# Attention with top-k and an MLP on one core: reads of the hidden products behind the score copies, GpSimd's part of the MLP later

## The chip, the cores and the metric

The kernel runs on one core of a Trainium2 chip. The metric is the device time of one execution in microseconds, as the median over several executions. A profiled execution gives, beside its own time, the span from its first to its last instruction and a record of every instruction on the engines: TensorE (PE, with its weight loads PEld), VectorE (DVE), ScalarE (ACT), GpSimd (POOL) and SyncE (SP), which issues the DMA transfers.

## The reference

For 8 batches and 8 heads, with 576 positions and 64 elements a head, attention keeps for every query the 32 largest scores. Its output, 4608 tokens of 512, goes through an MLP with a smoothed ReLU (SmeLU, beta 1) of width 2048. All is float32.

```python
scores = scale * np.matmul(q, k.transpose(0, 1, 3, 2))
kth = np.partition(scores, -top_k, axis=-1)[..., -top_k:-top_k + 1]
scores = np.where(scores >= kth, scores, -1000000000.0)
attn = np.exp(scores - np.max(scores, axis=-1, keepdims=True))
attn = attn / (np.sum(attn, axis=-1, keepdims=True) + 1e-09)
x = np.matmul(attn, v)          # then (B,H,S,D) -> (B*S, H*D)
h = x @ w_in
g = np.where(h >= 1, h, np.where(h <= -1, 0.0, (h + 1) ** 2 / 4))
out = g @ w_out
```

## The kernel before

**Steps.** Attention is cut into 144 steps. A step holds 128 queries of two heads, as two halves of a tile with 576 scores each. Four steps (the four pairs of heads) complete one chunk of 128 tokens for the MLP; there are 36 chunks. The order of four engines (TensorE, VectorE, ScalarE, GpSimd) is written out by hand: the Python loop over steps `m`, with 7 slots in each, issues the instructions, and every engine runs its own in that order. SP's order is left to the scheduler.

**One step.** TensorE makes the scores `sp` (L358) in two halves, each in a PSUM tile of tag "a", of which there are two. ScalarE copies them to `s` (L359). VectorE finds the 32nd largest: pairwise maxima and minima of the two halves of a row (`more` and `less`, L372), rounds of eight maxima and replacements (L392, L420, L428, L439, L446, L379), and a merging scan `kth` (L451). ScalarE makes the exponentials `e` (L395) from the negative maximum `nmax` (L393). VectorE masks them and sums them (L458), and takes the reciprocal `rz` (L404) early in the next step. GpSimd multiplies `e` by it (L411, twice a step) and writes two columns of `excess` (L414). ScalarE splits the weights into 16-bit halves (L488), SP stores them and reads them back transposed as `wT` (L490, L492), TensorE multiplies with the values into `po` (L506), and ScalarE copies that to the chunk's `xT` (L519).

**The MLP.** For each chunk, `hidden(x)` makes eight matrix products into one PSUM tile `ph` (L539), then ScalarE reads it twice, into `r` (L543) and `g` (L550), then GpSimd bounds `r` to 1 (L555), squares it (L556) and adds it to `g` (L557). There are two buffers of `r` and eight of `g`. `po` shares the three PSUM tiles of `ph`. `final(f)` multiplies `g` with `w_out` into `py` (L562), and comes four groups of `hidden` later (`LAG`); at the end ScalarE copies `y` (L565) and SP stores it.

**What sets the order around the change.** The MLP's pieces wait in a list `pending`. At the end of each slot `advance` takes pieces from it, as many as a share worked out from the work left allows, by planned costs and not by measured ones. In slot 2 of every even step, after the early steps in which weights are converted, the scores of two later steps are issued with the value products of two earlier steps between them (L794 to L800). Ahead of them a loop (L796) takes pieces until the last one is not a `hidden`. The divisions of the step before (L411) are issued in slot 0.

A second program for other input values is built after the first and started by a flag (L844). It isn't executed here.

Of the kernel before, what the change touches and what calls it, by code (L numbers as in the profile page):

```python
# [17 lines left out]
ALU = mybir.AluOpType  # L18
# [8 lines left out]
def kernel(  # L27
# [10 lines left out]
    nc = tc.nc  # L38
# [17 lines left out]
    GROUP = 2  # L56
# [51 lines left out]
    n_pieces = NK * DFF // WC + NF * DM // WC  # L108
# [68 lines left out]
    def run(ctx, paired):  # L177
# [350 lines left out]
            return [(i * TL, (i + 1) * TL, out[r0 + i * S + SM:r0 + (i + 1) * S, :]) for i in range(2)]  # L528

        def mlp(xT, rows, pool, last):  # L530
            gs, group = {}, 1 if last else GROUP
            py = []

            def hidden(x):
                ph = ps.tile([P, group, P], F32, name="ph", tag="ph", bufs=3)
                for i in range(group):
                    f = x * group + i
                    for kk in range(NK):
                        nc.tensor.matmul(ph[:, i], w_in[:, kk, f * P:(f + 1) * P], xT[:, kk],  # L539
                                         start=(kk == 0), stop=(kk == NK - 1))  # L540

                r = pool.tile([P, GROUP, P], F32, name="r", bufs=2)[:, 0:group]
                nc.scalar.activation(r, ph, AF.Relu, bias=half, scale=0.5 * unit)  # L543
                gs[x] = g = pool.tile([P, GROUP, P], F32, name="g", bufs=2 * LAG)[:, 0:group]
                if last:
                    nc.scalar.activation(g, ph, AF.Relu, bias=minus_half, scale=0.5 * unit)
                    nc.vector.scalar_tensor_tensor(out=r, in0=r, scalar=1.0, in1=r, op0=ALU.min, op1=ALU.mult)
                    nc.vector.tensor_tensor(out=g, in0=r, in1=g, op=ALU.add)
                    return
                nc.scalar.activation(g, ph, AF.Relu, bias=minus, scale=unit)  # L550
                if converted < n_pieces and x % 2:
                    nc.scalar.activation(r, r, AF.Square)
                    nc.gpsimd.tensor_scalar(r, r, 1.0, 0.0, ALU.min, ALU.max)
                else:
                    nc.gpsimd.tensor_scalar(r, r, 1.0, 0.0, ALU.min, ALU.max)  # L555
                    nc.gpsimd.tensor_tensor(out=r, in0=r, in1=r, op=ALU.mult)  # L556
                nc.gpsimd.tensor_tensor(out=g, in0=r, in1=g, op=ALU.add)  # L557

            def final(f):
                if f == 0:  # L560
                    py.append(ps.tile([P, DM], F32, name="py", tag="py", bufs=1))
                nc.tensor.matmul(py[0], gs[f // group][:, f % group], w_out[:, f, :], start=(f == 0), stop=(f == NF - 1))  # L562
                if f == NF - 1:
                    y = (late or words).tile([P, DM], F32, name="y", bufs=1)
                    nc.scalar.activation(y, py[0], AF.Copy, scale=unit)  # L565
                    for p0, p1, dst in rows:
                        nc.sync.dma_start(out=dst, in_=y[p0:p1])

            behind = []
            while pending and pending[-1][3]:
                behind.insert(0, pending.pop())
            for x in range(NF // group + LAG):
                if x < NF // group:
                    pending.append((NK * group, needed(x * group + group - 1, False), partial(hidden, x), False))
                if x < LAG:
                    for _ in range(min(GROUP + 1, len(behind))):
                        pending.append(behind.pop(0)[0:3] + (False,))
                else:  # L580
                    for f in range((x - LAG) * group, (x - LAG + 1) * group):
                        pending.append((DM // P, needed(f, True), partial(final, f), x >= NF // group))
# [14 lines left out]
        n = len(steps)  # L597
# [6 lines left out]
        pending = deque()  # L604
        total, spent = len(chunks) * (NK * NF + NF * DM // P), 0
        converted, inspected, due = 0, 0, 0.0

        begun, pipe = 0, deque()

# [23 lines left out]
        taken = None  # L633

        def take():

            nonlocal spent, due, pe_time, taken
            cost, pieces, work, _ = pending[0]
            if pieces > converted or usable[pieces] > pe_time + 0.5:
                return False  # L640
            pending.popleft()
            due -= cost
            spent += cost
            pe_time += cost * UNIT_TIME
            work()
            taken = work.func
            return True
# [62 lines left out]
        def begin_until(m):  # L710
            for x in range(len(state), m + 1):
                begin_at(x)
# [31 lines left out]
        for m in range(n + 2):  # L744
            early = converted < n_pieces
# [21 lines left out]
            for slot in range(SLOTS):  # L767
                now = start + (dve_time - start) * (slot + 1) / SLOTS
                for _ in range(parts[slot]):
                    next(top_k, None)  # L770
                if m < n and converted < n_pieces:
                    if slot in now_converting:
                        convert(now)
                elif slot == 3 and late is not None:
                    if m % 2:
                        inspect()
                    elif paired:
                        load(late, inspected, 1, 2)
                if slot == 1 and 1 <= m <= n and state[m - 1]["by_tensor"]:
                    pe_time = max(pe_time, done[m - 1] + 2.0) + 1.0  # L780
                    transpose_w(state[m - 1])
                    ready_at[m - 1] = pe_time + 1.8
                if slot == 3 and 1 <= m <= n and state[m - 1] is not None and not state[m - 1]["by_tensor"]:
                    move_w(state[m - 1])
                    ready_at[m - 1] = done[m - 1] + 15.0
                if slot == 3:
                    finish_turns()
                if slot == 2 and m == n and paired:
                    judge(ps, att)
                if slot == 2 and (early or m == first_late or m >= n - 1):  # L790
                    values_until(m)
                if m == 0 and slot in (1, 2):
                    next(first)
                if slot == 2 and not early:  # L794
                    if m % 2 == 0:
                        while pending and taken is not None and taken.__name__ == "hidden" and take():  # L796
                            pass
                    begin_until(min(m + 2, len(state)))
                    values_until((m - 2) // 2 * 2)
                    begin_until(m + 3 - m % 2)  # L800
                if slot == 4 and early:
                    begin_at(m + 2)
                if slot == (6 if early else 1):
                    queries(m + (3 if early else 5))
                    if (m < n and prep is None and next_keys < B and steps[m][0] == next_keys - 1 and steps[m][1] >= 1
                            and (next_keys > 1 or converted == n_pieces)):
                        prep = (turned_keys_of if next_keys > 1 else keys_of)(next_keys)
                    if prep is not None and (m % 2 == 0 or next_keys == 1):
                        got = next(prep, None)
                        pe_time += 0.5 if next_keys < 2 else 0.0  # L810
                        if got is None:
                            prep, next_keys = None, next_keys + 1
                        else:
                            keys[next_keys] = got
                            value_loads = got.get("loads", value_loads)
                    elif value_loads is not None:
                        next(value_loads, None)
                if paired and early and spent == 0 and not pending:
                    rest = ps.tile([P, NT, P], F32, name="rest", tag="py", bufs=1)
                    for i in range(5):  # L820
                        nc.tensor.transpose(rest[:, i % NT, :], ident, ident)
                advance((EARLY_SHARE if early else share) / SLOTS if m < n else 32.0, now)
            for _ in (top_k if top_k is not None else ()):
                pass
        while pending:
            advance(32.0, pe_time + 8.0)
        order.__exit__(None, None, None)


# [12 lines left out]
    with ExitStack() as inner:  # L842
        run(inner, True)
# [31 lines left out]
```

## Time and profile before

| what | us |
|---|---|
| median of 3 executions | 1488.8 (1488.8 to 1494.17) |
| profiled execution, own time | 1492.76 |
| its span | 1490.9 |
| TensorE busy | 1437.7 |
| VectorE busy | 1411.9 |
| ScalarE busy | 1157.7 |
| GpSimd busy | 949.8 |
| step to step in the middle, four steps | 37.77 to 38.60 |

Busy time is the union of an engine's instructions. Matrix products are pipelined and their ends are modelled, so that TensorE's busy time can hold short pauses. In rows of groups the columns are: line, engine, operation, output and inputs with sizes, count, busy us, mean ns of one, and idle time of the engine just before them with what ended it. In rows of the timeline they are: start, length, engine, line, operation, names, sizes, count, and in brackets the idle time before with its releaser.

### The profile page before, as it was taken

What the parts mean: (1) busy time and instruction counts of PE and PEld (TensorE: products, weight loads), DVE (VectorE), ACT (ScalarE), POOL (GpSimd) and SP (SyncE); (2) the same over time, 40 slices, a digit from 0 to 9 for tenths busy, and PEclk for the clock granted to TensorE, in tenths of its full rate; (3) what the DMA queues carried; (4) which work ended last, traced back from release to release, by engine and by line L of the source; (5) the groups of instructions that cost most, each with busy time, mean ns of one, the idle gap of its engine ahead of it and who ended that gap; (6) DMA issues with size and microseconds to landing.
All of it is one profiled execution on the core that took longest, in us unless ns stands there. A gap on an engine that the chain in (4) does not pass through costs nothing.

```text
span 1490.9 us, 32088 instructions
## 1 busy us (share of the span) xinstructions
PE 1437.7 (96%) x10755; PEld 1044.0 (70%) x10755; DVE 1411.9 (95%) x4392; ACT 1157.7 (78%) x2221; POOL 949.8 (64%) x1310
## 2 busy tenths in 40 slices
PE   7998899999999999999999999999999999999998
PEld 5765677777777777677767776767777777777675
DVE  6989999999999999999999999999999999999912
ACT  7986877888788877787778888788778887777632
POOL 3474576666676666666766667666666666677730
PEclk8999999999999999999999999999999999999999
DMA  8533567766677777886667786887677876665400
GB/s 253 193 120 107 149 170 203 198 182 170 170 202 197 192 184 204 204 209 177 170 186 199 198 200 173 208 214 182 170 201 187 203 202 168 161 167 138 149 25 17
DMA packets 510319, 260.94 MB, mean 175 GB/s; under 512 B 460992, under 2 KB 469184, under 8 KB 510144
## 3 DMA queue, kind: packets, MB, share of 16 engines
q1 hardware_dynamic: 510144, 258.80, 66.0%
q8 instruction: 87, 1.43, 0.4%
q14 instruction: 88, 0.72, 0.2%
HBM read 62.91 MB, written 102.63 MB: 111 GB/s over the span
## 4 chain that ended last, share of the span: by engine, by line
PE 65%; DVE 13%; ACT 10%; DMA 5%; POOL 4%; issue 3%; SPq 0%; POOLq 0%; ACTq 0%; DVEq 0%
PE py L562 26%; PE ph L539 23%; PE sp L358 8%; PE po L506 6%; DVE more L379 3%; ACT halves L488 2%; DVE e L458 2%; DMA rows<-halves 2%; ACT e L395 2%; POOL r L556 2%; DMA wT<-rows 2%; ACT r L543 1%; DVE more L372 1%; POOL g L557 1%; DVE tops L420 1%
## 5 line engine op out<-in xcount | busy, mean ns | idle before, releaser
L539 PEld LDWEIGHTS ph<-xT,w_in 128*128 128x128 f32 x4608 | 547.1, 192 | 102.3 <-issue 78.6
L539 PE MATMUL ph<-xT,w_in 128*128 128x128 f32 x4608 | 555.6, 276 | 2.3 <-ACT g L550 1.4
L562 PE MATMUL py<-w_out,g 128*128 128x512 f32 x1152 | 542.3, 597 | 0.7 <-ACT y L565 0.7
L555 POOL TENSOR_SCALAR r<-r 128x256 f32<-128x256 f32 x276 | 172.4, 625 | 401.3 <-ACT r L543 401.3
L379 DVE MATCH_REPLACE8 more<-tops,more 128x288 f32<-128x288 f32 x864 | 375.0, 437 | 0.0
L562 PEld LDWEIGHTS py<-w_out,g 128*128 128x128 f32 x1152 | 199.5, 191 | 165.1 <-issue 159.8
L488 ACT COPY halves<-e 128x1152 uint16<-128x1152 uint16 x268 | 293.7, 1143 | 19.9 <-DMA rows<-halves 12.5
L411 POOL TENSOR_SCALAR e<-e,rz 128x576 f32<-128x576 f32 x268 | 251.6, 949 | 10.0 <-DVE rz L404 10.0
L458 DVE SCALAR_TENSOR_TENSOR e<-s,kth,e 128x577 f32<-128x577 f32 x288 | 252.5, 912 | 0.5 <-ACT e L395 0.4
L543 ACT ACTIVATE r<-ph,half 128x256 f32<-128x256 f32 (+1 forms) x296 | 135.9, 459 | 145.2 <-PE ph L539 101.5
L557 POOL TENSOR_TENSOR g<-r,g 128x256 f32<-128x256 f32 x280 | 221.0, 789 | 22.0
L395 ACT ACTIVATE e<-s,nmax 128x576 f32<-128x576 f32 x288 | 222.6, 773 | 4.7
L556 POOL TENSOR_TENSOR r<-r 128x256 f32<-128x256 f32 x276 | 201.6, 730 | 23.0
L359 ACT ACTIVATE s<-sp 128x576 f32<-128x576 f32 x288 | 171.6, 649 | 52.6 <-PE sp L358 51.7
L358 PE MATMUL sp<-kT,qT 64*128 64x288 f32 x1024 | 163.9, 438 | 18.0 <-ACT s L359 12.4
L358 PEld LDWEIGHTS sp<-kT,qT 64*128 64x128 f32 x1024 | 89.0, 189 | 91.7 <-issue 35.3
L506 PE MATMUL po<-wT,v_in 128*64 128x128 f32 x2048 | 138.3, 276 | 6.4 <-DMA wT<-rows 5.6
L506 PEld LDWEIGHTS po<-wT,v_in 128*64 128x64 f32 x2048 | 113.2, 137 | 30.7 <-issue 11.4
L372 DVE TENSOR_TENSOR more<-s 128x576 f32<-128x576 f32 x144 | 122.5, 850 | 8.3 <-ACT s L359 8.3
L550 ACT ACTIVATE g<-ph,minus 128x256 f32<-128x256 f32 x280 | 129.8, 464 | 0.0
L420 DVE MAX8 tops<-more 128x8 f32<-128x288 f32 x288 | 125.4, 443 | 0.0
L392 DVE MAX8 tops<-more 128x8 f32<-128x288 f32 x288 | 116.4, 443 | 0.0
(92 smaller groups left out, 1378.3 us busy)
## 6 DMA issues: line engine op xcount, KB each, us to landing
rows<-halves SPq DMA_DIRECT2D x134, 576.0 KB, 3.4
lines<-parts SPq DMA_DIRECT2D x48, 256.0 KB, 2.7
q_in<-in_q_dram SPq DMA_DIRECT2D x32, 256.0 KB, 3.9
v_in<-in_v_dram SPq DMA_DIRECT2D x32, 256.0 KB, 4.3
out_dram<-y SPq DMA_DIRECT2D x32, 256.0 KB, 4.1
raw<-in_moe_w_in_dram SPq DMA_DIRECT2D x32, 256.0 KB, 3.3
raw<-in_moe_w_out_dram SPq DMA_DIRECT2D x32, 256.0 KB, 3.5
kT<-in_moe_w_in_dram SPq DMA_DIRECT2D x8, 512.0 KB, 4.8
```

The lines of the kernel that those rows point to most:

```text
L358: nc.tensor.matmul(*x, start=True, stop=True)
L379: nc.vector.match_replace(out=st["rest"][:, i, :], in_to_replace=eight(st["tops"], i, r - 8), in_values=src[:, i, :], imm_value=LOWEST)
L395: nc.scalar.activation(e[:, i, :], s[:, i, :], AF.Exp, bias=nmax[:, i:i + 1])
L411: nc.gpsimd.tensor_scalar(st["e"][:, i, :], st["e"][:, i, :], rz[:, i:i + 1], 1.0, ALU.mult, ALU.mult)
L458: nc.vector.scalar_tensor_tensor(out=st["all"][1][:, i, :], in0=st["all"][0][:, i, :], scalar=last[i], in1=st["all"][1][:, i, :], op0=ALU. ...
L488: nc.scalar.copy(halves[:, :, i * S:(i + 1) * S], st["e"][:, i, :].bitcast(U16).rearrange("p (k t) -> p t k", t=2))
L506: nc.tensor.matmul(po[j * D:(j + 1) * D], v_in[:, h, c, :] if c < NT else v_tl[0][:, h, :], wT[:, block(j, c)], start=(c == 0), stop=(c == ...
L539: nc.tensor.matmul(ph[:, i], w_in[:, kk, f * P:(f + 1) * P], xT[:, kk], start=(kk == 0), stop=(kk == NK - 1))
L555: nc.gpsimd.tensor_scalar(r, r, 1.0, 0.0, ALU.min, ALU.max)
L556: nc.gpsimd.tensor_tensor(out=r, in0=r, in1=r, op=ALU.mult)
L557: nc.gpsimd.tensor_tensor(out=g, in0=r, in1=g, op=ALU.add)
L562: nc.tensor.matmul(py[0], gs[f // group][:, f % group], w_out[:, f, :], start=(f == 0), stop=(f == NF - 1))
```

## The change

`hidden` no longer issues ScalarE's two reads itself: it puts them into a list `reads`, which is emptied at once unless `holding` is set. `holding` is set in slots 1 and 2 of even steps after the early ones, until the scores of slot 2's first `begin_until` are issued; then the held reads follow. The loop that takes pieces ahead of the scores stops when three reads are held. GpSimd's three instructions become `bound`, which goes to a queue `bounds`. An entry is issued at the end of a slot when more than two further slots have been done since it was made, or before the next read when more than one is queued, or when a `final` needs its `g`; in early steps and after the last attention step at the end of each slot. Arithmetic and instruction counts stay as they are.

```diff
             def hidden(x):
...
+                reads.append(partial(read, x, ph))
+                if not holding:
+                    issue_reads()
+
+            def read(x, ph):
+                while len(bounds) > 1:
+                    bounds.popleft()[1]()
                 r = pool.tile([P, GROUP, P], F32, name="r", bufs=2)[:, 0:group]
                 nc.scalar.activation(r, ph, AF.Relu, bias=half, scale=0.5 * unit)
                 gs[x] = g = pool.tile([P, GROUP, P], F32, name="g", bufs=2 * LAG)[:, 0:group]
...
                 nc.scalar.activation(g, ph, AF.Relu, bias=minus, scale=unit)
-                if converted < n_pieces and x % 2:
+                by_act = converted < n_pieces and x % 2
+                if by_act:
                     nc.scalar.activation(r, r, AF.Square)
-                    nc.gpsimd.tensor_scalar(r, r, 1.0, 0.0, ALU.min, ALU.max)
-                else:
-                    nc.gpsimd.tensor_scalar(r, r, 1.0, 0.0, ALU.min, ALU.max)
+                bounds.append((slots_done, partial(bound, x, r, g, by_act)))
+
+            def bound(x, r, g, by_act):
+                nc.gpsimd.tensor_scalar(r, r, 1.0, 0.0, ALU.min, ALU.max)
+                if not by_act:
                     nc.gpsimd.tensor_tensor(out=r, in0=r, in1=r, op=ALU.mult)
                 nc.gpsimd.tensor_tensor(out=g, in0=r, in1=g, op=ALU.add)
+                whole_g.add(x)
 
             def final(f):
...
+                if f // group not in gs:
+                    issue_reads()
+                while f // group not in whole_g:
+                    bounds.popleft()[1]()
...
+        def issue_reads():
+            while reads:
+                reads.pop(0)()
...
+                holding = not early and m % 2 == 0 and slot in (1, 2) and m < n
                 if slot == 2 and not early:
                     if m % 2 == 0:
-                        while pending and taken is not None and taken.__name__ == "hidden" and take():
+                        while len(reads) < 3 and pending and taken is not None and taken.__name__ == "hidden" and take():
                             pass
                     begin_until(min(m + 2, len(state)))
+                    holding = False
+                    issue_reads()
                     values_until((m - 2) // 2 * 2)
                     begin_until(m + 3 - m % 2)
...
                 advance((EARLY_SHARE if early else share) / SLOTS if m < n else 32.0, now)
+                slots_done += 1
+                while bounds and (early or m >= n or bounds[0][0] < slots_done - 2):
+                    bounds.popleft()[1]()
...
         while pending:
             advance(32.0, pe_time + 8.0)
+            while bounds:
+                bounds.popleft()[1]()
```

More of the change, by code (lines that the diff above doesn't have):

```diff
@@ L530, in mlp @@
         def mlp(xT, rows, pool, last):
-            gs, group = {}, 1 if last else GROUP
+            gs, group, whole_g = {}, 1 if last else GROUP, set()
             py = []
@@ L548, in hidden @@
                     nc.vector.tensor_tensor(out=g, in0=r, in1=g, op=ALU.add)
+                    whole_g.add(x)
                     return
                 nc.scalar.activation(g, ph, AF.Relu, bias=minus, scale=unit)
-                if converted < n_pieces and x % 2:
+                by_act = converted < n_pieces and x % 2
+                if by_act:
                     nc.scalar.activation(r, r, AF.Square)
-                    nc.gpsimd.tensor_scalar(r, r, 1.0, 0.0, ALU.min, ALU.max)
-                else:
-                    nc.gpsimd.tensor_scalar(r, r, 1.0, 0.0, ALU.min, ALU.max)
+                bounds.append((slots_done, partial(bound, x, r, g, by_act)))
+            def bound(x, r, g, by_act):
+                nc.gpsimd.tensor_scalar(r, r, 1.0, 0.0, ALU.min, ALU.max)
+                if not by_act:
                     nc.gpsimd.tensor_tensor(out=r, in0=r, in1=r, op=ALU.mult)
                 nc.gpsimd.tensor_tensor(out=g, in0=r, in1=g, op=ALU.add)
+                whole_g.add(x)
             def final(f):
@@ L606, in run @@
         converted, inspected, due = 0, 0, 0.0
+        reads, bounds, holding, slots_done = [], deque(), False, 0
+        def issue_reads():
+            while reads:
+                reads.pop(0)()
         begun, pipe = 0, deque()
```

## The prediction

> **What bounds the kernel now.** I read the page first, then waits by engine in the steady middle, then two equal stretches side by side, then the instructions of one of them.
>
> ```profile
> PE 1437.7 (96%) x10755; PEld 1044.0 (70%) x10755; DVE 1411.9 (95%) x4392; ACT 1157.7 (78%) x2221; POOL 949.8 (64%) x1310
> ```
>
> TensorE (PE) and VectorE (DVE) are both nearly full, so the page alone doesn't say which sets the end. The waits from 200 to 1410 us do: VectorE has none at all, and TensorE has this one of size (us in total, times, longest), while ScalarE (ACT) waits often for TensorE and for GpSimd (POOL):
>
> ```profile
> PE sp L358 <- ACT s L359: 10.4, 16, 1.4
> ACT r L543 <- POOL g L557: 36.1, 26, 2.3
> ```
>
> So VectorE's own instructions, back to back, carry the time from about 170 us to 1420 us, and nothing that shortens a wait elsewhere can shorten that, unless VectorE's instructions themselves get shorter. They can. L458, L372 and L451 of VectorE have these durations (min/median/max ns):
>
> ```profile
> L458 DVE SCALAR_TENSOR_TENSOR e<-s,kth,e x288: 799/811/1815, 25.8 to 1420.8; 128x577 f32<-128x577 f32 x144
> L451 DVE TENSOR_TENSOR_SCAN kth<-tops,seconds x144: 190/200/1269, 25.3 to 1419.7; 128x25 f32<-128x25 f32 x144
> ```
>
> From 200 to 1410 us the means are 912 ns for L458 (x252) and 846 and 805 ns for the two forms of L372 (x126 each, median 746); L451 has 289 over the whole run. Mean less median: 252 x 0.101 = 25.5 us, 126 x (0.100 + 0.059) = 20.0 us, 126 x 0.089 = 11.2 us, together 57 us in 126 steps, or 0.45 us a step. What lengthens them stands in the timeline below: GpSimd runs at that moment.
>
> Four attention steps make one period, with one chunk of MLP in it. Two pairs of periods (us, then busy us of PE, PEld, DVE, ACT, POOL):
>
> ```profile
> 752.46:791.06 38.60, 37.91 (x274) 27.23 (x273) 38.60 (x121) 30.01 (x59) 26.93 (x37) 1.00 0.70 194
> 791.06:829.65 38.59, 37.89 (x273) 27.21 (x273) 38.59 (x121) 31.87 (x61) 26.92 (x37) 1.00 0.72 193
> 1023.45:1061.22 37.77, 37.77 (x274) 27.30 (x273) 37.77 (x121) 30.60 (x59) 24.15 (x36) 1.00 0.70 172
> ```
>
> The same work takes 38.6 us in one and 37.77 in the other. TensorE's busy time is the same within 0.14 us; the long period has 0.69 us of TensorE idle. 37.77 is thus about what TensorE needs with no stall. From the reciprocal at 205.05 us to that at 1395.91 there are 31 periods in 1190.86 us, mean 38.41; if all took 37.77 the stretch would be 1170.9, 20 us less. That is the most the change can give there while TensorE does the same work.
>
> The place of the 0.69 us, in the second of these periods: ScalarE, TensorE, GpSimd, VectorE.
>
> ```profile
> 817.08 0.47 ACT L543 ACTIVATE r<-ph,half 128x256 f32<-128x256 f32 x1 [1.13 <-POOL g L557]
> 817.81 1.19 ACT L359 ACTIVATE s<-sp 128x576 f32<-128x576 f32 x2
> ...
> 818.51 1.30 PE L358 MATMUL sp<-kT,qT 64*128 64x288 f32 x8 [0.70 <-ACT s L359]
> ...
> 814.50 1.74 POOL L556 TENSOR_TENSOR r<-r 128x256 f32<-128x256 f32 x1
> 816.31 0.73 POOL L557 TENSOR_TENSOR g<-r,g 128x256 f32<-128x256 f32 x1
> 818.89 1.97 POOL L411 TENSOR_SCALAR e<-e,rz 128x576 f32<-128x576 f32 x2
> ...
> 818.28 0.70 DVE L451 TENSOR_TENSOR_SCAN kth<-tops,seconds 128x25 f32<-128x25 f32 x1
> 819.31 0.93 DVE L458 SCALAR_TENSOR_TENSOR e<-s,kth,e 128x577 f32<-128x577 f32 x1
> 820.18 1.29 DVE L458 SCALAR_TENSOR_TENSOR e<-s,kth,e 128x577 f32<-128x577 f32 x1
> ```
>
> The third read of hidden products waits for a free r (two buffers, the first still with GpSimd, whose L556 took 1.74 us against a usual 0.61 because VectorE's two L372 ran). The score copies stand behind that read, though their products were done at 815.5; the next scores find no bank and TensorE waits. Over on VectorE, L451 loses 0.50 us, and L458 0.12 and 0.48, to GpSimd's L557 and the two L411.
>
> **What the Trainium skill says.** "SBUF — State Buffer", section "Who interferes with whom": a VectorE instruction with two SBUF inputs contends with a GpSimd instruction that reads SBUF; whichever issues first holds the pair for its whole length and the other blocks. The trace agrees: L372, L451 and L458 all have two inputs and stretch, and GpSimd's L556 stretches to 1.74 when it comes second. VectorE's maxima and replacements, with one input, keep 437 to 443 ns as group means. "PSUM — Partial Sum Buffer", section "Engine vs sequencer instructions": the queues of ScalarE, VectorE and GpSimd are strict first in, first out. The trace agrees: copies whose input was done at 815.5 start at 817.81, behind the read.
>
> **The change part by part.** No instruction is added or removed on any engine. The orders of TensorE and VectorE are the same in both programs. In the program that runs, ScalarE's order changes in 33 places, once in four steps: one pair of reads (r and g, 0.47 us each; two pairs at the first place) goes behind two score copies and ahead of the copies of po. GpSimd's changes in 33 places: the last of three parts "bound" (0.40 + 0.61 + 0.73 = 1.74 us alone) goes behind the two L411 and L414 of the step. Most other bounds keep their rank, because a bound is delayed only past what is issued within three slots, and that is mostly nothing. On SP one key load changes place with one row store and one weight load with one transposition, once each, where the first rows are stored (around 170 us). Such transfers land in 2.8 to 4.7 us, and both moved ones feed later steps, so I put them at nothing; if the keys or the weights came late, it would cost one such landing, 5 us at most.
>
> ScalarE's move, in the period shown: ScalarE is free at 815.95, the scores done at 815.48, so the copies run 815.95 to 817.14 and not 817.81 to 819.00. The second scores can start when po ends, at 817.81: the 0.70 us are gone. The third read follows at 817.14 (r is free at 817.04) and ends at 818.0, hardly later than now; the copies of po come 0.9 us earlier. Behind the held read stand only those; the next products that need its bank start at 820.70, so 2 us cover it. Without the cover TensorE would wait what the read is late. Sum over the middle: 10.4 us of TensorE's stalls, 16 of them.
>
> GpSimd's move: L411 starts at 817.04 instead of 818.89, 1.85 us earlier (its reciprocal was done at 811.65). Alone it takes 2 x 0.74, to 818.5. VectorE's L451 at 818.28 then waits 0.23 instead of 0.50. L414 and the moved bound come next, 818.7 to about 820.7, and now they meet L458: I take up to 0.2 for the first and 0.35 for the second (what is left of L556's 0.61 when VectorE's own changeover is taken off, as L411's 0.74 costs 0.48 in the rows above). Sum 0.8 against 1.1: 0.3 us less. Bounds of this unknown: 0.7 less, if the moved bound always comes second to VectorE; 0.4 more, if it also pushes the following bound, now starting at 824.6, in front of L372. I take 0.3, since a bound is shorter than an L411. x 33 = 10 us on VectorE. What the moved bound makes late is its g, by about 2.4 us; its py stands four groups later, in periods with eight groups, some 19 us, which hides it. Its r is wanted by the read at 823 to 824 and free near 820.8.
>
> Both sums are about 10 us, on the two engines that pace each other, so they do not add: 10 us come off. The profiled execution has a span of 1490.9 and a time of 1492.8, 1.9 more; it would go to 1482.8. It lies 4.0 above the median of the runs shown, between 1488.8 and 1494.17, so from the median: 1488.8 - 10 = 1478.8, said as 1479. The last 70 us, with VectorE nearly done, and the first 160, where weights are converted, keep their order and their time.
>
> **The rivals.** *Full recovery:* with the stalls gone, TensorE runs ahead of VectorE until L411 ends before L372 in every step; then VectorE falls under 37.77 and TensorE sets the pace: 20 us less, 1469. For it: the long and short periods differ only in how the engines lie to each other. Against: VectorE has no wait at all even in the short ones.
>
> *Contention only moves:* VectorE sets the end alone, and what L451 no longer loses L458 and L372 lose to the moved bound; TensorE's stall was cover that VectorE never felt: 1489, give or take 5. For it: VectorE never waited on the scores that come earlier. Against: L411 is the longest GpSimd instruction in these collisions and it leaves the place where they are worst.
>
> *Slower:* TensorE's loop, freed of its 0.70 us, carries GpSimd earlier against VectorE. In the second and third step of the period the reciprocals end at 792.5 and 802.0, L372 starts at 795.22 and 804.72, and L411 comes just behind it (795.69, 805.26) and yields. If GpSimd comes more than 0.5 us earlier, L411 is first, and L372 waits up to 0.74 once or twice instead of the 0.37 and 0.44 now: about 0.4 more a step, 0.8 a period, less the 0.3 above: 0.5 x 31 = 15 us more, 1504. It decides if the lead settles between 0.5 and 1.5 us; past 1.5, L411 is through before L372 begins. For it: the stall removed is larger than 0.5. Against: a lead that makes VectorE slower grows further, and leaves the bad stretch.
>
> **How the numbers follow.** Forecast (8 to 13 us less) 0.40, full recovery (over 13) 0.15, contention only moves 0.28, slower 0.17. Half a per cent, 7.4 us, is about what a measurement of this kernel can tell from no change: faster 0.55, same 0.28, slower 0.17. The likeliest time is 1479, its own range 1475 to 1482. The range for 8 in 10 runs from full recovery, 1470, to just past no change, 1496, and leaves out most of the slower rival and the extreme of the recovery. It takes in 0.7 less a period (1466 if TensorE let it, which it doesn't) and, in part, 0.4 more (1502).
>
> **What would show it.** Right: TensorE's wait for the score copies falls from 10.4 us to under 2; ScalarE's wait of reads for GpSimd stays near 36; L411 starts about 1.9 us earlier in the fourth step; the mean of L451 falls under 0.25 us; VectorE still has no waits, and periods are near 38.1. Wrong: VectorE's means of L372 rise over 0.88 (the slower rival), or the 57 us of contention stay while the stall goes (it only moves), or VectorE starts to wait for scores (full recovery).

## The result, and the profile after

The changed kernel takes 1482.18 us (median of 6, 1478.1 to 1484.11) against 1490.64 us (median of 6, 1488.8 to 1494.17): ratio 0.9936, 95% interval 0.9918 to 0.9953, or 8.5 us less of a forecast 10. The profiled executions have spans of 1490.9 and 1482.2 us.

The first part of the page after (busy us, share of the span, instructions):

```profile
PE 1435.8 (97%) x10755; PEld 1044.6 (70%) x10755; DVE 1403.9 (95%) x4392; ACT 1158.0 (78%) x2221; POOL 926.6 (63%) x1310
```

VectorE is busy 8.0 us less and TensorE 1.9 us less, with the same instructions. Of TensorE's waits from 200 to 1410 us, and then ScalarE's for GpSimd there (us in total, times, longest), these are the two longest of TensorE and those that answer to the ones shown of before (L550 is now the first read, L567 and L568 are the square and the addition):

```profile
PE po L514 <- DMA wT<-rows: 3.0, 2, 1.9
PE po L506 <- ACT parts L283: 2.5, 1, 2.5
...
PE sp L358 <- ACT s L359: 0.7, 1, 0.7
...
ACT r L550 <- POOL g L568: 3.4, 5, 1.0
ACT r L550 <- POOL r L567: 2.6, 2, 1.3
```

TensorE's wait for the copies went from 10.4 to 0.7 us. Not all of that is gain: its other waits, for transposed weights (`wT`) and for the parts of keys that ScalarE makes (L283) above all, grew from 4.1 to 7.5 us between 200 and 1380 us, so that its waits there fell by 6.3 us, from 14.5 to 8.2. The 1.9 us of busy time go with a granted clock of 0.992 in the profile after and 0.991 before.

Now the same place in a period of the changed kernel: ScalarE, TensorE, GpSimd, VectorE.

```profile
847.33 1.04 ACT L283 COPY parts<-k_block 128x1024 uint16<-128x1024 uint16 x1
848.26 1.20 ACT L359 ACTIVATE s<-sp 128x576 f32<-128x576 f32 x2
849.50 0.47 ACT L550 ACTIVATE r<-ph,half 128x256 f32<-128x256 f32 x1
...
849.85 0.39 PE L506 MATMUL po<-wT,v_tail 128*64 128x128 f32 x4
850.17 1.24 PE L358 MATMUL sp<-kT,qT 64*128 64x288 f32 x8
...
846.93 1.73 POOL L567 TENSOR_TENSOR r<-r 128x256 f32<-128x256 f32 x1
848.74 0.73 POOL L568 TENSOR_TENSOR g<-r,g 128x256 f32<-128x256 f32 x1
849.45 1.47 POOL L411 TENSOR_SCALAR e<-e,rz 128x576 f32<-128x576 f32 x2
...
850.70 0.28 DVE L451 TENSOR_TENSOR_SCAN kth<-tops,seconds 128x25 f32<-128x25 f32 x1
851.31 0.81 DVE L458 SCALAR_TENSOR_TENSOR e<-s,kth,e 128x577 f32<-128x577 f32 x1
852.05 1.16 DVE L458 SCALAR_TENSOR_TENSOR e<-s,kth,e 128x577 f32<-128x577 f32 x1
```

GpSimd's square is held as long as before (1.73 us; VectorE's two L372 ran from 846.77), but the copies no longer stand behind the read that waits for it: they follow L283, and the second scores start where `po` ends, without a wait. L411 starts 5.52 us after the reciprocal (843.93), with 5.53 forecast and 7.38 before. VectorE loses 0.08 on L451 and 0.35 on the second L458, where it lost 1.1.

From the reciprocal at 202.28 us to that at 1385.19 there are again 31 periods, 38.16 us each (38.41 before). About the last ten run at what the prediction called TensorE's need, as these two do (us, then busy us of PE, PEld, DVE, ACT, POOL; the third number from the end is the granted clock):

```profile
1082.99:1120.76 37.77, 37.77 (x273) 27.29 (x273) 37.77 (x122) 30.12 (x60) 25.02 (x36) 1.00 0.77 200
1120.76:1158.53 37.77, 37.77 (x273) 27.29 (x273) 37.77 (x121) 31.80 (x62) 25.04 (x36) 1.00 0.74 192
```

The longest of the others takes 40.73 us. It holds a wait of 2.52 us for the parts of the keys, and behind it a stretch in which TensorE was granted little more than half its clock:

```profile
639.00:642.40 3.40, 3.40 (x26) 2.08 (x22) 3.40 (x11) 1.79 (x5) 2.94 (x4) 0.57 0.69 261
```

### The profile page after: what moved, and what is told of

It reads as the page before. It is cut to its first block, busy times and chain, and to the rows that moved or that the text cites. A ratio compares the mean times of both kernels' runs of the same rounds, so it can differ in the third digit from the quotient of the medians.

```text
span 1482.2 us, 32086 instructions
## 1 busy us (share of the span) xinstructions
PE 1435.8 (97%) x10755; PEld 1044.6 (70%) x10755; DVE 1403.9 (95%) x4392; ACT 1158.0 (78%) x2221; POOL 926.6 (63%) x1310
## 4 chain that ended last, share of the span: by engine, by line
PE 80%; DVE 10%; DMA 4%; ACT 4%; issue 2%; SPq 1%; ACTq 0%; DVEq 0%
PE ph L539 30%; PE py L578 29%; PE sp L358 9%; PE po L506 9%; DVE more L379 2%; DMA rows<-halves 2%; DVE e L458 2%; DMA wT<-rows 1%; PE po L514 1%; DVE more L372 1%; DVE tops L420 1%; DVE tops L428 1%; DVE tops L392 1%; PE pw L473 1%; ACT halves L488 1%
## 5 line engine op out<-in xcount | busy, mean ns | idle before, releaser
L565 POOL TENSOR_SCALAR r<-r 128x256 f32<-128x256 f32 x280 | 166.9, 596 | 413.4 <-ACT r L550 409.7
L568 POOL TENSOR_TENSOR g<-r,g 128x256 f32<-128x256 f32 x280 | 241.6, 863 | 22.0
L458 DVE SCALAR_TENSOR_TENSOR e<-s,kth,e 128x577 f32<-128x577 f32 x288 | 246.9, 893 | 0.1
L411 POOL TENSOR_SCALAR e<-e,rz 128x576 f32<-128x576 f32 x268 | 235.9, 890 | 13.2 <-DVE rz L404 13.2
L550 ACT ACTIVATE r<-ph,half 128x256 f32<-128x256 f32 (+1 forms) x296 | 136.1, 460 | 107.8 <-PE ph L539 99.7
L567 POOL TENSOR_TENSOR r<-r 128x256 f32<-128x256 f32 x276 | 183.1, 663 | 23.0
L372 DVE TENSOR_TENSOR more<-s 128x576 f32<-128x576 f32 x144 | 124.1, 862 | 6.0 <-ACT s L359 6.0
L420 DVE MAX8 tops<-more 128x8 f32<-128x288 f32 x288 | 125.4, 443 | 0.0
L372 DVE TENSOR_TENSOR less<-s 128x576 f32<-128x576 f32 x144 | 117.7, 817 | 0.0
```

Of the source, the lines that this page charges most:

```text
L372: nc.vector.tensor_tensor(out=x, in0=s[:, :, 0:SH], in1=s[:, :, SH:S], op=op)
L411: nc.gpsimd.tensor_scalar(st["e"][:, i, :], st["e"][:, i, :], rz[:, i:i + 1], 1.0, ALU.mult, ALU.mult)
L458: nc.vector.scalar_tensor_tensor(out=st["all"][1][:, i, :], in0=st["all"][0][:, i, :], scalar=last[i], in1=st["all"][1][:, i, :], op0=ALU. ...
```

## The experiments

Two causes were left side by side by the prediction: TensorE's stall at the scores (A), and GpSimd's divisions leaving the place where they lengthen VectorE's instructions (B). Ratios are to the kernel before on the same chip, with 95% intervals. "Stall" is TensorE's wait for the score copies from 200 to 1380 us (10.4 us before), and "all waits" is the sum of its waits there (14.5 us before). These and the busy times are of one profiled execution each; the ones of the changed kernel, act_only and after_r3 were the slowest of their six.

| run | ratio | interval | stall | all waits | VectorE busy |
|---|---|---|---|---|---|
| changed kernel | 0.9936 | 0.9918 to 0.9953 | 0.7 | 8.2 | 1403.9 |
| act_only | 0.9937 | 0.9916 to 0.9957 | 0.8 | 10.1 | 1404.2 |
| pool_only | 0.9937 | 0.9918 to 0.9956 | 4.3 | 8.4 | 1403.1 |
| before_r3 | 0.9942 | 0.9922 to 0.9962 | 1.6 | 8.6 | 1402.2 |
| after_r3 | 0.9928 | 0.9907 to 0.9948 | 0 | 10.4 | 1403.3 |
| after_write_only | 0.9921 | 0.9896 to 0.9945 | 0.5 | 7.5 | 1353.5 |
| before_write_only | 0.9921 | 0.9895 to 0.9946 | 1.4 | 7.1 | 1357.7 |
| after_dve_less | 0.9925 | 0.9901 to 0.9949 | 0 | 7.3 | 1391.4 |
| before_dve_less | 0.9995 | 0.9981 to 1.0008 | 5.6 | 11.5 | 1388.7 |
| before_r3_dve | 0.9935 | 0.9918 to 0.9952 | 0.7 | 7.4 | 1372.7 |
| after_pe_less | 0.9883 | 0.9859 to 0.9907 | 1.2 | 21.2 | 1401.4 |
| before_pe_less | 0.9953 | 0.9940 to 0.9966 | 7.7 | 26.3 | 1408.1 |
| after_pe_less_wo | 0.9806 | 0.9778 to 0.9834 | 0 | 15.7 | 1353.9 |

**Each part alone.** In act_only ScalarE has the changed order and GpSimd the old one; in pool_only it is the other way round. The orders of TensorE and VectorE are the same in all four.

```diff
 act_only, against the changed kernel
-                bounds.append((slots_done, partial(bound, x, r, g, by_act)))
+                bound(x, r, g, by_act)
 pool_only, against the changed kernel
-                holding = not early and m % 2 == 0 and slot in (1, 2) and m < n
+                holding = False
```

> ScalarE's order of the changed kernel, GpSimd's order of the kernel before: the reads are held, each bound is issued with its read. Theory A (the gain comes from TensorE's stall at the scores): the stall of 10.4 us goes, time 8 to 9 us under before, like the whole change. Theory B (the gain comes from GpSimd's L411 leaving the place where it blocks L451 and L458): the stall goes too, but VectorE's means of L451 (289 ns) and L458 (912) stay, and the time stays within 3 us of before.

> GpSimd's order of the changed kernel, ScalarE's order of the kernel before: no read is held, bounds come later. Theory A: TensorE's wait for the score copies stays near 10 us and the time within 3 us of before. Theory B: mean of L451 falls to about 233 ns as in the changed kernel, VectorE is busy 6 to 8 us less, time 6 to 9 us under before, stall or not.

Each part alone brings the whole gain, within what intervals of 3 us either way can tell, so neither theory stands as it was put. ScalarE's part does what A said, and VectorE is busy 7.7 us less in it although GpSimd's order is the old one; that already speaks against B. GpSimd's part leaves 4.3 of the 10.4 us of stall, yet its time can't be told from the others'; all of TensorE's waits together are 8.4 us in it, about as many as in the changed kernel. Its mean of L451 is 264 ns from 200 to 1380 us, not the 233 that B expected, and the same as in act_only.

**The wait for r taken away, in the old orders.** Three buffers of `r`, and seven of `g` for room, in the kernel before and in the changed one.

```diff
-                r = pool.tile([P, GROUP, P], F32, name="r", bufs=2)[:, 0:group]
+                r = pool.tile([P, GROUP, P], F32, name="r", bufs=3)[:, 0:group]
...
-                gs[x] = g = pool.tile([P, GROUP, P], F32, name="g", bufs=2 * LAG)[:, 0:group]
+                gs[x] = g = pool.tile([P, GROUP, P], F32, name="g", bufs=2 * LAG - 1)[:, 0:group]
```

> The kernel before with three buffers of r instead of two (and seven of g instead of eight, for room); all orders as before. The third read no longer waits for GpSimd. Theory A: TensorE's stall falls under 2 us and the time falls like that of the ScalarE part alone, 8 us. Theory B: the stall falls, L411 keeps its place behind three bounds, L451 and L458 stay as long, time within 3 us of before.

> The changed kernel with three buffers of r and seven of g. Its stall at the scores is already 0.7 us, so theory A gives nothing more, within 2 us of the changed kernel. Theory B: nothing either, unless the freer reads shift GpSimd against VectorE; 0 to 4 us either way.

One more buffer gives the kernel before what the reordering gives, with no instruction moved, and gives the changed kernel nothing more that could be measured. The third read's wait for `r` is thus enough as the root of the loss. B said within 3 us of before: wrong, although L411 is where it was in GpSimd's order.

**GpSimd with almost nothing to read.** The three instructions of a bound and the two divisions of a step become fills of the same tiles, so that bounding, squaring, adding and dividing are left out. Only L414, of two columns, still reads.

```diff
-                    nc.gpsimd.tensor_scalar(st["e"][:, i, :], st["e"][:, i, :], rz[:, i:i + 1], 1.0, ALU.mult, ALU.mult)
+                    nc.gpsimd.memset(st["e"][:, i, :], 0.001)
...
-                nc.gpsimd.tensor_scalar(r, r, 1.0, 0.0, ALU.min, ALU.max)
+                nc.gpsimd.memset(r, 0.5)
                 if not by_act:
-                    nc.gpsimd.tensor_tensor(out=r, in0=r, in1=r, op=ALU.mult)
+                    nc.gpsimd.memset(r, 0.25)
-                nc.gpsimd.tensor_tensor(out=g, in0=r, in1=g, op=ALU.add)
+                nc.gpsimd.memset(g, 0.5)
```

> The changed kernel with GpSimd's three instructions of a bound and its two divisions of a step replaced by fills of the same tiles (nothing is read; the bounding, squaring, adding and dividing are left out); orders as changed. VectorE then meets no reader but L414: its means go to L451 0.20, L458 0.81, L372 0.74 us. If TensorE's work (37.77 us a period) is the floor, the time falls 8 to 14 us under the changed kernel, to about 1470. If VectorE alone sets the pace, it falls by the whole contention, 50 us, to about 1430.

> The same fills in the kernel before, orders as before. If what the change removes is lost only through the port that VectorE and GpSimd share, this one is as fast as the changed kernel with fills, within 2 us, the stall at the scores included, since L556 is then never held. If the order of ScalarE has a worth of its own, it stays 5 to 10 us slower than that.

VectorE's work falls by 50 us and the time stays at that of the changed kernel, in either order. 1430 us didn't come, nor 1470: the 31 periods take 38.0 us each in after_write_only, and only some 18 of them lie near 37.77. VectorE now waits openly, which it did neither in the kernel before nor in the changed one:

```profile
DVE e L458 <- ACT e L395: 38.8, 45, 3.3
```

This is after_write_only from 200 to 1380 us. So the 50 us by which GpSimd lengthened VectorE's instructions in the changed kernel did not set its time. And with GpSimd hardly ever held, the order of ScalarE has no worth of its own: both versions have the ratio 0.9921.

**Less of VectorE's work.** One of the two maxima of `less` is left out in each step (for one half of the tile the merging scan then reads a list that isn't renewed), in both kernels.

```diff
-                for i in range(2):
+                for i in range(1):
                     nc.vector.max(out=seconds[:, (1 - i) * SPLIT + 1:(1 - i) * SPLIT + 9], in_=st["less"][:, i, :])
```

> The changed kernel with one of the two maxima of less in each step left out (L446, 144 x 0.37 = 53 us of VectorE). TensorE's pace: no more than 12 us less than the changed kernel, periods at 37.77. VectorE's pace: 45 to 53 us less.

> The kernel before with the same maximum left out (53 us of VectorE). If VectorE set the pace before the change: 40 us or more under before. If TensorE with its stalls sets it and VectorE only follows: VectorE's instructions grow longer against GpSimd by about what was taken, and the time lies between the changed kernel's (0.994 of before) and before's, by how much of the 10.4 us stall is left where the engines then lie.

Taking 53 us from the engine that never waits brings nothing in either kernel. In the changed one VectorE's busy time falls only from 1403.9 to 1391.4 us: some 40 of the 53 us come back as longer instructions. From 200 to 1380 us, L458 and L451 there (count | busy us, mean ns | idle before):

```profile
L458 DVE SCALAR_TENSOR_TENSOR e<-s,kth,e 128x577 f32<-128x577 f32 x250 | 238.6, 989 | 1.7 <-ACT e L395 1.6
...
L451 DVE TENSOR_TENSOR_SCAN kth<-tops,seconds 128x25 f32<-128x25 f32 x124 | 48.5, 391 | 0.0
```

and the same two rows of the changed kernel with its full work:

```profile
L458 DVE SCALAR_TENSOR_TENSOR e<-s,kth,e 128x577 f32<-128x577 f32 x248 | 213.2, 895 | 0.0
...
L451 DVE TENSOR_TENSOR_SCAN kth<-tops,seconds 128x25 f32<-128x25 f32 x123 | 28.5, 232 | 0.0
```

The kernel before without the maximum is not as fast as the changed one without it: 0.9995 against 0.9925. Its waits from 200 to 1380 us show what a readier VectorE does to the old order:

```profile
ACT r L543 <- POOL g L557: 29.4, 25, 1.9
ACT r L543 <- POOL r L556: 12.5, 10, 1.4
...
PE sp L358 <- ACT s L359: 5.6, 17, 0.4
```

And its chain of waits in one period of the middle (start, us, what) goes through the read that waits for GpSimd into the copies and the scores:

```profile
770.54 0.45 ACT r L543
771.06 0.69 POOL r L555
771.84 1.00 POOL r L556
772.91 0.74 POOL g L557
773.68 0.47 ACT r L543
774.15 0.36 ACT g L550
774.51 0.55 ACT s L359
775.11 1.30 PE sp L358 x8
```

In after_dve_less ScalarE's reads wait 2.7 us for GpSimd, and TensorE never for the copies. In before_dve_less TensorE's waits sum to 11.5 us in the middle, 3 less than the 14.5 of before, and yet the time is the same to 0.1%. Between these two profiles 1.6 us of the 3 are lost again before 200 us, where TensorE is idle for 29.6 us instead of 27.9, and 1.0 in its busy time (1438.8 against 1437.7, at a granted clock of 0.990 against 0.991). Why they are lost there isn't shown.

**Both, to close it.** The kernel before with three buffers of `r` and without the maximum:

> The kernel before with three buffers of r (seven of g), and with the maximum left out (53 us of VectorE). With two buffers the maximum's absence gave nothing (0.9995). If what held TensorE there is the third read's wait for r and the copies behind it, this one is at the floor that the changed kernel has without the maximum: ratio 0.991 to 0.995, no wait of TensorE for the copies. If VectorE's collisions hold TensorE in another way, it stays near 0.999.

0.9935. With the wait for `r` gone, the missing maximum again makes nothing better, but the loss to 0.9995 is gone too. That loss therefore came through the wait for `r`.

**Less of TensorE's work.** The product `f = 7` of each chunk is left out, so that `y` lacks one of 16 terms.

```diff
-                nc.tensor.matmul(py[0], gs[f // group][:, f % group], w_out[:, f, :], start=(f == 0), stop=(f == NF - 1))
+                if f != 7:
+                    nc.tensor.matmul(py[0], gs[f // group][:, f % group], w_out[:, f, :], start=(f == 0), stop=(f == NF - 1))
```

> The changed kernel without one of the 16 last products of a chunk (f = 7 is left out, 36 x 0.43 = 15.5 us of TensorE). TensorE's pace: 8 to 15 us less than the changed kernel. VectorE's pace: only the products after VectorE's end count, about 1 to 2 us less.

> The kernel before without the product f = 7 (15.5 us of TensorE). If TensorE with its stalls sets the pace: 6 to 15 us under before. If the loop of ScalarE and GpSimd around the third read sets it, TensorE's waits grow by what was taken and the time stays within 4 us of before.

> The changed kernel without the product f = 7 and with the fills on GpSimd. Without the product alone the ratio to before was 0.988 and not 0.983, that is 6 us and not 15.5. If VectorE, lengthened by GpSimd, is the next limit there, the rest comes now: ratio 0.981 to 0.984, about 1466 to 1469. If something else is (ScalarE, transfers), it stays at 0.988.

The 15.5 us of the expectations are half of what was left out. The rows of the product in the changed kernel and in after_pe_less show 72 instructions less, two for each of 36 products, and 31 us:

```profile
L578 PE MATMUL py<-w_out,g 128*128 128x512 f32 x1152 | 541.5, 597 | 1.8 <-ACT y L581 1.8
...
L579 PE MATMUL py<-w_out,g 128*128 128x512 f32 x1080 | 510.6, 597 | 4.1 <-ACT y L582 4.1
```

Of these 31 us the kernel before gives back 7.0 (0.0047 x 1490) and the changed one, set against its own ratio, 7.9 (0.9936 to 0.9883). So TensorE's work counts, where 53 us of VectorE's brought nothing; but after a quarter of it something else holds the kernel. In after_pe_less TensorE waits 21.2 us in all instead of 8.2, 16.2 of them for transposed weights, and its granted clock is lower: 0.985 in the profile instead of 0.992, and 0.983 to 0.987 in all four executions. The clock alone costs TensorE an estimated 10 us (0.007 of 1478). Why it is lower isn't shown. ScalarE waits for VectorE's maxima, from 200 to 1380 us:

```profile
ACT nmax L393 <- DVE tops L392: 57.1, 52, 2.6
```

This was 17.3 us in the changed kernel, so VectorE is likely to be the next limit. With the fills the wait is 0.9 us, and the ratio goes from 0.9921 to 0.9806 by the missing product: 17 us, more than half of the 31. But the fills lighten GpSimd as well as VectorE, and the granted clock was higher too (0.986 to 0.991), so VectorE's part in the rest is argued and not shown.

No experiment points to a version that is faster than the changed kernel with the same work: more buffers gave nothing on top, and less contention gave nothing either while TensorE has its full work.

## Why the prediction was right, and where not

**The time** was forecast at 1479, 10 us less; it is 1482.18, 8.5 us less, just above the narrower of the two ranges (1475 to 1482). The kernel before itself measured 1490.64 over the runs that go with it, 1.8 more than the median that the forecast started from.

**ScalarE's move** was worked out right. The copies follow L283, the second scores start at the end of `po`, and the stall of 10.4 us is gone but for 0.7. act_only shows that this alone brings the whole gain. What the sum left out is that TensorE's other waits would grow, by 3.4 us.

**GpSimd's move** was right in place: L411 came 1.86 us earlier against the reciprocal, with 1.85 forecast. VectorE's loss there was put at 0.8 us and is 0.43 in the step shown. The mean of L451 was to fall under 0.25 us; it fell from 0.289 to 0.232. That isn't this move's doing alone: the mean is 0.264 with the move alone, and 0.264 and 0.257 without it, in act_only and before_r3.

**The step that failed** is the first: that VectorE's instructions, back to back without a wait, carry the time. VectorE's 53 us less changed nothing in either kernel, and 50 us less of contention changed nothing in the changed one. TensorE's work with its stalls carries it, as long as none of that work is taken away. The 8 us by which VectorE is less busy follow from TensorE's shorter time, as they do in act_only and before_r3, where GpSimd's order is the old one. The "10 us on VectorE" is no cause of its own; that it came out like TensorE's 10.4 was chance. The view that could have told is the two periods side by side: VectorE was full in 37.77 us and full in 38.60 with the same work, so its length was not its own, while TensorE's differed by just the stall.

**That the sums do not add** held: either part alone gives all of it. GpSimd's part does so with 4.3 us of stall left, but all of TensorE's waits together sum to 8.4 us there, 8.2 in the changed kernel and 10.1 in act_only. What the others no longer wait at the scores, they wait in part for transposed weights and parts of keys. How a later bound shortens the stall in pool_only isn't shown.

**ScalarE's wait of reads for GpSimd** was said to stay near 36 us and fell to 3.4 for the addition, or with the square from 38.4 to 6.0. The prediction's own walk had the answer: it put the held read at 817.14 and `r` free at 817.04.

**The rivals.** "Contention only moves" took VectorE for the engine that sets the end, and falls with that. Its sign, 57 us of contention that stay, didn't come either: the same sum of means less medians is 49 us in the changed kernel, and the 8 us between them are those by which VectorE is less busy. "Full recovery" describes about the last third of the run, with its periods near 37.8, but not the mean of 38.16. "Slower" didn't come: the means of L372 rose from 846 and 805 to 860 and 826 ns, under the 0.88 us named.

## What to carry to other kernels

An engine without a wait need not be the one that sets the pace: where two engines hold each other up, as VectorE and GpSimd do here, the one with time to spare may spend it inside its instructions, which get longer, and the profile then shows it full. Take work from it before believing it, and count in the trace how much was taken and whether the granted clock stayed: here one product was twice the instructions that were expected. And where a read that waits for a buffer stands in a queue ahead of a copy that the busiest engine needs, try one more buffer, or the copy placed first. Here either brought 8 to 9 us where that engine had waited 10.4 for the copies, and its other waits grew.

## What the runs showed of the hardware

VectorE's freed time turned for three quarters into contention: of an estimated 53 us taken away (144 x 0.37) it was only 12.5 us less busy, with no more than 1.6 us of new waits from 200 to 1380 us. GpSimd's fills, which read nothing, left VectorE's instructions near their lengths alone in either order: L451, L458 and the two L372 have means of 202, 816, 749 and 752 ns in after_write_only and of 203, 818, 751 and 754 in before_write_only, against medians of 198, 812, 748 and 747 in the changed kernel. The fills keep GpSimd busy for 460.9 us in after_write_only, and VectorE's busy time fell by 50.4 us.

TensorE's busy time depends on the clock that it is granted. Eight products of the scores took 2.29 us at 640.23, in the stretch with a granted clock of 0.57, and 1.24 us at 850.17. With the same instructions TensorE is busy for 1434.7 us in after_dve_less, at a mean clock of 0.992, and for 1441.4 us in after_r3, at 0.989.
